# The order of work in a fused recurrence and MLP: first units from the third on, and the repeated unit

## The chip, the cores and the metric

The kernel runs on one core of a Trainium2 chip. The metric is the time of one execution on the device in microseconds (us); of several executions the median is taken. The five engines are called TensorE (PE in the profile; PEld is its loading of weights), VectorE (DVE), ScalarE (ACT), GpSimd (POOL) and SyncE (SP). Each works off its own instructions in the order in which the program issues them. Transfers are issued from the queues of SP, ScalarE and GpSimd, each in order too.

## The reference

Two blocks follow each other. The first is a recurrence over 768 time steps, for 4 batches and 8 heads of size 48, with a gate for every element of the key:

```
f = 1 / (1 + exp(-f_logit))
for t in range(S):
    state = f[t, :, None] * state + outer(k[t], v[t])      # 48 x 48 for each batch and head
    y[t]  = q[t] @ state
```

The heads' outputs are laid side by side to x of shape 4 x 768 x 384. The second block is a layer norm without offset and an MLP with a residual:

```
xn  = (x - mean) / sqrt(var + 1e-6) * g_ln
out = x + relu(xn @ w_ch1) @ w_ch2          # 384 -> 1536 -> 384
```

Everything is in float32 but the two weight matrices, which arrive as 64-bit floats; the kernel turns them into 32-bit ones on the chip.

## The kernel before

**Units.** Time is cut into 12 units of 64 steps. A unit holds all four batches, so 256 tokens, and all eight heads. `attention(n)` makes x of unit n, `mlp(n)` its result. The recurrence inside a unit becomes matrix products: running products of the gates forwards and backwards (two scans on VectorE), keys and queries multiplied by them, scores between them with a causal mask, scores times values, and the queries times the state that the earlier units left.

**Stages of attention**, each a name in the plan, with n the unit:

- gates (L691): sigmoid of the gates on ScalarE. For units 0 to 2 TensorE transposes the raw gates first. From unit 3 on (`DIRECT`) the data comes transposed by a transfer: `split` (words p and P, L421) copies the raw data on ScalarE into two planes of 16-bit halves and writes them to DRAM, and `transfer` (word x, L443) reads them back transposed, always on SP's queue. The tile `turned` takes the gates and later the queries of a unit.
- after and upto (L666, L675): the two scans; k and q (L712, L721): the keys times after (kh), the queries times upto (qh); kept (L732): the state times the unit's total gate.
- carried (L749, products at L758): queries times kept state, into the PSUM tile py; scores (L772) and causal (L778).
- kt (L788): kh transposed. From unit 3 on this is a transfer on SP that reads the halves of kh (word with K), which ScalarE (L440) and the queue have written before.
- values (L808): masked scores times v, added into py, and three copies on ScalarE that make x (L817, L819). chunk (L846): kt times v, the new part of the state, into the PSUM tile `shared`, which the scores use as well. state (L854): the sum of kept state and new part, on VectorE.
- stats, norm (L831 to L835, L876): mean and variance, and xn. turn (L887, L889): six transposes of xn on TensorE and six copies on ScalarE that multiply by g_ln and make xt.

**The MLP in steps.** `mlp(n)` is a generator, and each word m runs one step. In unit 0 the first product is made in halves by `first_half` (words h). Units 0 to 2 multiply plainly by w1 (L1023), units 0 and 1 plainly by w2 (L1033, six steps each). From unit 3 on the first product is made of 15 block products (`by_blocks`, L952), with sums of blocks of xt (`sums_of_x`, word y, L922, on VectorE) and sums of blocks of w1 (`mix_first`, words u for VectorE and U for GpSimd, L612, 13 steps in all). From unit 2 on the second product is made of seven products (L1052, named p1, p2, p6, p5, p7, p3, p4 in their order) with sums of blocks of h (`sums`, word s, L931 to L934) and of w2 (`mix`, words t and T, L586). Each product is followed by additions on VectorE and GpSimd (L1060) and by stores of results on SP. A unit from 3 on thus has 22 steps m.

**Weights.** Words f, r and w fetch a piece of a weight matrix (SP), unpack it (ScalarE, L547) and put it together (VectorE L556 to L561, GpSimd L563).

**Loads.** l and L load one of f, k, q, v of a unit, on SP's queue or ScalarE's, in four transfers (L475).

**What sets the order.** There is no planner at run time. Two strings hold it: START for the first units and UNIT, which is repeated for m = 3 to 11 with n = m + 1, o = m + 2, p = m + 3, z = m + 4. `run` goes through the words and issues each one's instructions; that order is every engine's order. Words of units that do not exist are passed over.

**PSUM.** py and shared have two banks each; the other four banks (`one_bank`) serve all other products and transposes in turn.

**A second path** (`general_path`) stands behind a condition for very small gates and is not taken with the reference's inputs.

## Time and profile before

| | |
|---|---|
| time, median of 3 runs | 431.71 us (430.95 to 435.05) |
| the profiled execution's own time | 433.26 us |
| its span, first to last instruction | 431.6 us |
| mean granted clock of TensorE | 0.992 |
| HBM read, written | 28.31 MB, 23.59 MB |

The page's first part gives each engine's busy time, its share of the span and its instructions. Its second part cuts the span into 40 slices of 10.8 us, a digit being the busy tenths. The waits name the engine and line that stood idle, what ended the wait, the sum in us, how often, and the longest. The chain of waits starts from the last instruction and goes back to what released it, or to the instruction before it on the same engine; in order of time it gives start, length and what it was. In a timeline each line is a start, a length, the engine, the line of the program, the operation, the tile written and the tiles read, the shape and the number of instructions; in brackets the idle time before it and what ended it. Queue lines (SPq, POOLq) are the issuing of transfers, not the transfers themselves. Lengths of neighbouring matmul groups overlap a little, since matmuls are pipelined.

### The profile page before, as it was taken

Reading aid. Unit: us, or ns where it says so; the run is one execution under the profiler, and the core shown is the slowest. Engines: PE = TensorE matmul, PEld = TensorE weight load, DVE = VectorE, ACT = ScalarE, POOL = GpSimd, SP = SyncE. Lnnn points to the kernel's source line nnn. Section 1 sums busy time; section 2 is a strip of 40 time slices with the busy share of each in tenths; the row PEclk is TensorE's granted clock in tenths of the full one; section 3 lists DMA queues with packets and bytes.
Section 4 is the critical chain, followed back from the end, with each engine's and each line's share of the span. In section 5 each row is a group of like instructions: output and inputs, shape, how many; then the busy total and the mean of one; then the engine's idle time right before and its main releaser. Section 6 shows DMA issues by size and latency. Waiting matters only on the chain.

```text
span 431.6 us, 12972 instructions
## 1 busy us (share of the span) xinstructions
PE 415.2 (96%) x5435; PEld 387.3 (90%) x5435; DVE 335.1 (78%) x539; ACT 215.3 (50%) x364; POOL 121.9 (28%) x148
## 2 busy tenths in 40 slices
PE   6599899999999999999999999999999999999994
PEld 5489787767879999999999999999999999999994
DVE  5999699769397779879879879878879878574561
ACT  2593786355243574573573573574583453341410
POOL 2351445832014115016016016025025024021020
PEclk9699999999999999999999999999999999999999
DMA  9998989857968698796796897897885782301001
GB/s 166 294 179 209 226 231 239 200 150 181 225 156 209 156 221 209 190 211 177 194 211 169 180 238 177 199 195 210 163 203 157 155 144 67 69 3 27 11 9 33
DMA packets 167647, 71.68 MB, mean 166 GB/s; under 512 B 151760, under 2 KB 157840, under 8 KB 167584
## 3 DMA queue, kind: packets, MB, share of 16 engines
q1 hardware_dynamic: 151728, 54.38, 58.4%
q0 software_dynamic: 3872, 12.64, 8.1%
q10 hardware_dynamic: 11984, 3.79, 4.2%
q8 instruction: 44, 0.72, 0.7%
q14 instruction: 19, 0.16, 0.1%
HBM read 28.31 MB, written 23.59 MB: 120 GB/s over the span
## 4 chain that ended last, share of the span: by engine, by line
PE 89%; DMA 4%; ACT 2%; DVE 2%; issue 1%; SPq 0%; ACTq 0%
PE pp L1052 32%; PE bx L952 11%; PE by L952 10%; PE ph L1023 7%; PE po L1033 7%; PE bz L952 4%; DMA w_0words<-in_moe_w_ch_dram 3%; PE py L808 3%; PE py L758 2%; PE shared L772 2%; PE ph L901 2%; PE bw L952 2%; PE bv L952 2%; PE xp L887 2%; PE shared L846 2%; DMA fraw<-in_f_logit_dram 1%
## 5 line engine op out<-in xcount | busy, mean ns | idle before, releaser
L963 ACT ACTIVATE h<-h 128x512 f32<-128x512 f32 x45 | 28.4, 630 | 42.0 <-DVE h L960 35.9
L1052 PE MATMUL pp<-mixed,h 128*128 128x192 f32 x240 | 42.3, 326 | 0.0
L1052 PE MATMUL pp<-w,h 128*128 128x192 f32 x240 | 40.9, 327 | 0.0
L1052 PE MATMUL pp<-mixed,s 128*128 128x192 f32 x240 | 40.6, 326 | 0.0
L1052 PEld LDWEIGHTS pp<-mixed,s 128*128 128x128 f32 x240 | 39.3, 190 | 0.0
L1052 PEld LDWEIGHTS pp<-w,h 128*128 128x128 f32 x240 | 38.8, 190 | 0.3
L1052 PEld LDWEIGHTS pp<-mixed,h 128*128 128x128 f32 x240 | 39.1, 190 | 0.0
L960 DVE TENSOR_TENSOR h<-h,bx 128x512 f32<-128x512 f32 x36 | 24.6, 683 | 18.1 <-PE bx L952 17.4
L669 DVE TENSOR_TENSOR_SCAN after<-gates,ends 128x1040 f32<-128x1040 f32 (+1 forms) x13 | 30.4, 2338 | 6.3 <-ACT gates L700 3.2
L440 ACT COPY Kplanes<-kh 128x1024 uint16<-128x1024 uint16 x18 | 18.1, 1044 | 34.2 <-DVE kh L717 31.1
L889 ACT ACTIVATE xt<-xp,gain 128x128 f32<-128x128 f32 x72 | 20.0, 378 | 28.9 <-PE xp L887 28.9
L1033 PE MATMUL po<-w,h 128*128 128x384 f32 x96 | 32.2, 487 | 0.0
L1023 PE MATMUL ph<-xt,w 128*128 128x256 f32 x144 | 31.8, 380 | 0.2 <-ACT xt L889 0.2
L1023 PEld LDWEIGHTS ph<-xt,w 128*128 128x128 f32 x144 | 27.2, 190 | 4.3 <-ACT xt L889 0.5
L834 POOL TENSOR_SCALAR rstd<-mv 128x2 f32<-128x2 f32 (+1 forms) x13 | 8.2, 627 | 76.3 <-DVE mv L832 76.1
L952 PE MATMUL bx<-y,v 128*128 128x128 f32 x216 | 28.9, 276 | 0.5 <-issue 0.4
L681 DVE TENSOR_TENSOR_SCAN upto<-gates,starts 128x1040 f32<-128x1040 f32 (+1 forms) x13 | 28.1, 2159 | 0.5
L1033 PEld LDWEIGHTS po<-w,h 128*128 128x128 f32 x96 | 17.9, 190 | 11.0
L441 POOL DMA_DIRECT2D qhalves<-qplanes x9 | 4.9, 544 | 79.5 <-ACT qplanes L440 79.5
L952 PEld LDWEIGHTS bx<-y,v 128*128 128x128 f32 x216 | 26.4, 192 | 0.8 <-issue 0.8
L563 POOL TENSOR_TENSOR w<-w_0upper,w_0units 128x768 int32<-128x768 int32 x7 | 15.0, 2139 | 25.6 <-DVE w_0upper L561 25.6
L440 ACT COPY kplanes<-kraw 128x1024 uint16<-128x1024 uint16 x18 | 18.1, 1045 | 8.0 <-DMA fhalves<-fplanes 3.2
(172 smaller groups left out, 962.7 us busy)
## 6 DMA issues: line engine op xcount, KB each, us to landing
w_0words<-in_moe_w_ch_dram SPq DMA_DIRECT2D x7, 768.0 KB, 6.4
v<-in_v_dram SPq DMA_DIRECT2D x46, 96.0 KB, 3.8
Khalves<-Kplanes POOLq DMA_DIRECT2D x16, 256.0 KB, 3.7
kraw<-in_k_dram SPq DMA_DIRECT2D x40, 96.0 KB, 3.5
fhalves<-fplanes POOLq DMA_DIRECT2D x14, 256.0 KB, 3.7
kraw<-in_q_dram SPq DMA_DIRECT2D x36, 96.0 KB, 3.1
fraw<-in_f_logit_dram ACTq DMA_DIRECT2D x27, 96.0 KB, 3.0
khalves<-kplanes SPq DMA_DIRECT2D x9, 256.0 KB, 2.6
```

The costliest lines, as they stand in the source:

```text
L440: nc.scalar.copy(out=to, in_=src)
L563: nc.gpsimd.tensor_tensor(out=to.bitcast(I32), in0=upper, in1=units, op=ALU.add)
L669: nc.vector.tensor_tensor_scan(out=at["after"].rearrange(flat)[:, c0:c1][:, ::-1], data0=gt[:, c0 + 1:c1 + 1][:, ::-1], data1=ends.rearran ...
L681: nc.vector.tensor_tensor_scan(out=at["upto"].rearrange(flat)[:, c0:c1], data0=gt[:, c0:c1], data1=starts.rearrange(flat)[:, c0:c1], initi ...
L808: nc.tensor.matmul(py[half(b ^ r), r, e * D:(e + 1) * D], lhsT=sc[half(b), r, e], rhs=vt[half(b), g, 2 * a + r], start=n == 0 and e == 0, ...
L889: nc.scalar.mul(out=xt[:, m, g * P:(g + 1) * P], in_=pt[:, m], mul=gain[:, m:m + 1])
L952: nc.tensor.matmul(banks[bank][:, i], lhsT=right[:, i * P:(i + 1) * P], rhs=left, start=new and i == 0, stop=True, skip_group_check=True)
L960: nc.vector.tensor_tensor(out=out[to], in0=out[to], in1=bank, op=op)
L963: nc.scalar.activation(out=out[to], in_=out[to] if bank is None else bank, func=AF.Relu)
L1023: nc.tensor.matmul(ph[:, j], lhsT=w1[:, m, (i + j) * P:(i + j + 1) * P], rhs=xt[:, m], start=m == 0, stop=m == KD - 1)
L1033: nc.tensor.matmul(po, lhsT=h[:, i, g * P:(g + 1) * P], rhs=w2[:, i], start=i == 0, stop=i == KF - 1)
L1052: nc.tensor.matmul(pp, lhsT=a[:, i], rhs=b[:, i], start=i == 0, stop=i == KH - 1)
```

## The change

Both strings are put in another order. Of START everything up to the word w that follows the fifth m1 stays; from there on, beginning with the query stage of unit 2 (a2.q), the words stand differently: among others a2.q, the load of unit 4's v (l4v), the mixing steps (t, u, U) and the steps m0, m1, m2 have other places. In UNIT the state's products (a{n}.chunk) stand before the values (a{n}.values); a{o}.upto and one of the splits of f stand one step m away from where they stood; a{o}.k stands before a{o}.q; the load of q stands a step earlier and the statistics a step later; and at the end one of the two K splits stands behind the turn, which itself stands one step m earlier. The words themselves, and how often each occurs, are the same.

```diff
 h01 r a1.kx h01 a1.carried a1.k l2f a1.scores w r a1.kt h00 a1.causal a1.values f w l2k
 a1.stats h00 f r a1.chunk a2.gates h01 a1.norm a1.turn l3f a2.kx f P3f0 m1 w r a2.after
 a2.k p3f1 a2.upto a1.state r l3k f a2.kept m1 P3k1 w m1 m1 r w l2v m1 w
-                                                                        p3k0 f m1 r x3f
-a3.gates a2.q l3q m0 m0 a2.carried L4f a2.scores a2.kt w a2.causal x3k P3q1 m1 u T
-a3.after U P3q0 L4k a2.values x3q a2.chunk U P4f1 m1 a3.k U a2.stats a2.norm P3K0 m0 m0
-u a2.state P4k1 m0 u a2.turn P4k0 t p3K1 m0 m2 l4q p4f0 a3.upto l3v a3.kept u u p4q0
-p4q1 m2 a3.q m2 u x4f u t l5f m1 a3.carried a3.scores m2 a4.gates m2 a3.causal m2 m1
-a3.values a4.after x4k a3.kt s2 x4q P5f0 a4.k P5f1 a3.chunk u a3.stats a3.state L5k l5v
-m2 a3.norm m1 p5k0 a4.upto l6f a4.q U p5k1 m1 x5f P4K1 l4v m2 m2 m2 U a3.turn l5q
-a5.gates p4K0 y3 m2 a4.kept m2 m2
+a2.q p3k0 f r m1 x3f m0 l3q P3q1 m0 x3k a2.carried a2.scores a3.gates a2.kt m1 w
+a2.causal P3q0 L4f a2.values a3.after L4k T P4f1 u a2.chunk m0 U x3q U U P4k1 a2.stats a3.k
+a2.norm P3K0 u m0 m1 a2.state m0 a2.turn p3K1 u m0 P4k0 t p4f0 l4q l3v m2 a3.upto a3.kept p4q1
+u p4q0 u m2 a3.q u m1 m2 t m2 a3.carried l4v a3.scores x4f m2 a4.gates u a3.causal m2 m1 a3.kt
+l5f a3.values a4.after s2 x4k x4q a4.k a3.stats u P5f1 a3.chunk L5k P5f0 p5k1 a3.state a3.norm
+a4.upto l5v m2 m1 p5k0 a4.q l6f m1 x5f m2 a4.kept P4K1 m2 l5q m2 m2 U a3.turn U a5.gates m2
+p4K0 m2 y3
 """
 UNIT = """
 a{n}.kt a{n}.carried p{p}f1 a{o}.after a{n}.scores m{m} a{n}.causal m{m} m{m} m{m} P{o}q0 m{m}
-m{m} m{m} m{m} m{m} a{o}.upto m{m} p{o}q1 p{p}f0 m{m} m{m} m{m} x{o}k a{n}.values l{p}k
-a{n}.chunk m{m} a{n}.stats m{m} x{o}q s{m} p{p}k1 P{p}k0 L{z}f a{o}.q a{o}.k m{m} x{p}f m{m}
-m{m} l{p}q l{p}v a{n}.norm m{m} m{m} a{n}.state m{m} p{o}K1 p{o}K0 a{n}.turn a{o}.kept y{n}
+m{m} m{m} m{m} a{o}.upto m{m} m{m} p{o}q1 m{m} p{p}f0 m{m} m{m} a{n}.chunk x{o}k a{n}.values
+l{p}k m{m} x{o}q m{m} a{n}.stats s{m} p{p}k1 a{o}.k P{p}k0 L{z}f a{o}.q m{m} x{p}f l{p}q m{m}
+m{m} l{p}v a{n}.norm m{m} m{m} a{n}.state p{o}K0 a{n}.turn m{m} a{o}.kept p{o}K1 y{n}
 a{p}.gates m{m}
 """
```

The lines are broken here where the two orders part; in the file the line breaks differ, the words do not.

## The prediction

> **What bounds the kernel now.** I read the page's busy rows first, then TensorE's waits (of the whole run, then from 84 us on), then the chain of waits in order of time.

> ```profile
> span 431.6 us, 12972 instructions
> PE 415.2 (96%) x5435; PEld 387.3 (90%) x5435; DVE 335.1 (78%) x539; ACT 215.3 (50%) x364; POOL 121.9 (28%) x148
> PE   6599899999999999999999999999999999999994
> ...
> PE shared L772 <- DVE qh L688: 5.2, 2, 3.7
> ...
> PE bx L952 <- issue: 0.4, 1, 0.4
> ...
> 206.34 1.08 PE py L758 x64
> 238.94 1.08 PE py L758 x64
> 270.92 1.08 PE py L758 x64
> 302.90 1.08 PE py L758 x64
> 335.26 1.08 PE py L758 x64
> 412.29 13.67 PE pp L1052 x84
> ```

> The third line is TensorE in 40 slices: the holes are at both ends. The longest wait, 5.2 us, belongs to the first units (line 688 serves only units 0 to 2). Asked from 84 us on, the view holds one line, the 0.4 us for the issue of a product. The chain says the same: from there on it runs over TensorE without a break, and the carried products (L758) that open each unit follow each other by 32.60, 31.98, 31.98 and 32.36 us. A unit is thus 31.98 us of TensorE work end to end, and two of these four are longer, by 0.62 and 0.38 us: 1.0 us in all, the 0.4 within it. The last product ends at 412.29 + 13.67 = 425.96, and the span's other 5.6 us are a last addition and a store.

> From where does the change act? The first word that differs is a2.q, ahead of unit 1's sixth product pair.

> ```profile
> 70.60 1.04 PE L661 MATMUL tr<-ident,qraw 128*128 128x128 f32 x8
> 72.26 1.28 DVE L688 TENSOR_TENSOR qh<-tr,upto 128x512 f32<-128x512 f32 x2
> 76.73 1.15 PE L758 MATMUL py<-kept,qh 48*64 48x48 f32 x64
> ```

> Its transposes stand at 70.60 us and move up by one product pair. Everything earlier, with nearly all of TensorE's idle time, keeps its order; what lies behind is TensorE from end to end. **No instruction is added or taken away: every word of both strings is there as often as before.** So the change can win back about 1.0 us at most, and can lose whatever wait it puts in front of TensorE.

> **The change, part by part.**

> *a2.q first.* On VectorE the queries' product stands behind a weight piece's conversion (w) in either order, at 72.26, and the carried products that need it come at 76.73, behind two products of unit 0 in either order: about 3 us of cover behind its end. Cost 0.

> *State's products (a{n}.chunk) ahead of the values, in the repeated unit.*

> ```profile
> 284.74 1.15 PE L808 MATMUL py<-v,sc 64*64 64x48 f32 x64
> 285.71 0.90 PE L846 MATMUL shared<-v,kt 64*48 64x48 f32 x64
> 286.54 1.16 PE L952 MATMUL by<-y,v 128*128 128x128 f32 x8
> 287.54 1.06 PE L952 MATMUL bx<-y,v 128*128 128x128 f32 x8
> 286.25 0.46 ACT L817 COPY x<-py 128x384 f32<-128x384 f32 x1
> 286.72 0.96 ACT L819 COPY x<-py 64x384 f32<-64x384 f32 x2
> 288.35 0.55 DVE L831 BATCH_NORM_STATS2 stats<-x 128x6 f32<-128x384 f32 x1
> ```

> The two groups stay neighbours behind the same 13 products. The 0.1 us that a group takes longer after a change of the tile's shape (1.16 against 1.06 for L952) falls on whichever comes first: 0, and at most 0.1 us a unit either way. The values end 0.83 us later (285.71 to 286.54), and ScalarE's copies of x with them. Those end now at 286.72 + 0.96 = 287.68 and the statistics start at 288.35, a cover of 0.67 us; but the first copy starts at 286.25, 0.5 us after the values gave way to the next group at 285.71, so some 0.4 of the 0.83 arrives. Cost 0; with the cover gone 0.2 us of VectorE a unit.

> *a{o}.k before a{o}.q; the load of q past a step.* The two products swap on VectorE and what follows them starts as now. On SP the four loads go ahead of two stores of results for which nothing waits. Cost 0.

> *The turn (transposes of the normalised x, L887) one product earlier, K1 behind it.* This shortens a cover. TensorE and VectorE in two units, and xn in an early one:

> ```profile
> 266.20 2.11 PE L1052 MATMUL pp<-w,s 128*128 128x192 f32 x12
> 264.96 1.13 DVE L876 TENSOR_SCALAR xn<-x,mv,rstd 128x384 f32<-128x384 f32 x2
> ...
> 298.18 2.11 PE L1052 MATMUL pp<-w,s 128*128 128x192 f32 x12
> 296.55 1.14 DVE L876 TENSOR_SCALAR xn<-x,mv,rstd 128x384 f32<-128x384 f32 x2
> 300.13 0.82 PE L887 MATMUL xp<-ident,xn 128*128 128x128 f32 x6
> ...
> 90.82 0.87 DVE L876 TENSOR_SCALAR xn<-x,mv,rstd 128x384 f32<-128x384 f32 x2 [2.39 <-POOL rstd L835]
> ```

> The transposes take the places at 266.20 and 298.18. xn is complete at 264.96 + 1.13 = 266.09 and at 297.69, so the cover shrinks, in the second unit from 300.13 - 297.69 = 2.44 us to 0.49, in the first to 0.11. The first three transposes need only xn's first half, which gives some 0.5 us more. I take 0.05 us for each of eight full units, 0.4 in all; the ends are 0 and 8 x 0.3 = 2.4 us, 0.3 being what xn is seen to vary by (0.87 there, 1.13 here). In return the copies of xt start 2 us ahead of now, which is worth 0 because y, made from them, is not late now. K1's copy falls behind the six xt copies, some 3 us:

> ```profile
> 299.12 1.41 POOL L441 DMA_DIRECT2D Khalves<-Kplanes  x2
> Khalves<-Kplanes POOLq DMA_DIRECT2D x16, 256.0 KB, 3.7
> 307.68 2.57 SPq L455 DMA_TRANSPOSE kt<-Khalves  x1
> ```

> The second half, issued at about 302.5 and landed 3.7 us later, is there at 306, and kt reads it at 307.68, on SP behind stores. Cost 0; were it late, SP would wait, behind it q's halves and the keys' transfer, and the state's products, which now come 13.8 us after the unit's opening (284.74 - 270.92), would lose of the 9 us that they come behind kt's issue.

> *The rest of START* moves products of units 0 to 2 against attention. The tight place is unit 4's gates: their transfer (x4f) now stands on SP behind a store of unit 1 and the four loads of unit 4's v.

> ```profile
> 108.37 0.55 DVE L1038 TENSOR_TENSOR x<-x,po 128x384 f32<-128x384 f32 x1 [0.51 <-PE po L1033]
> 102.36 2.77 SPq L475 DMA_DIRECT2D v<-in_v_dram  x4
> 106.03 2.91 SPq L455 DMA_TRANSPOSE turned<-fhalves  x1
> DMA to landing us min/median/max: 6.0/6.0/6.0
> turned<-fhalves SPq DMA_TRANSPOSE x9, 4.4
> 113.68 1.05 ACT L696 ACTIVATE gates<-turned 128x1024 f32<-128x1024 f32 x1
> 118.99 0.96 DVE L931 TENSOR_TENSOR s<-h 128x768 f32<-128x768 f32 x1 [1.91 <-ACT h L1025]
> 133.27 0.54 DVE L1038 TENSOR_TENSOR x<-x,po 128x384 f32<-128x384 f32 x1
> 135.70 0.82 PE L887 MATMUL xp<-ident,xn 128*128 128x128 f32 x6
> ```

> The store's addition (108.37, after 0.51 us of waiting for its product, which comes earlier now) stands behind as much VectorE work as now, so at about 107.9 and done at 108.4. About 1 us for the store and 2.8 for the loads (as at 102.36): x4f at 112 and landed, 6.0 us later as the one at 106.03 was, at 118; gates done at 119, now at 114.73. From there VectorE has the list it has now, up to the addition that ends at 133.27 + 0.54 = 133.81: 19.1 us, of which 1.9 are the wait at 118.99, which the delay swallows. So it is done at 119 + 17.2 = 136.2. It frees the PSUM bank of unit 2's product p7 (my reading, if banks go out in the order in which they come free), and p7 takes the transposes' place at 135.70. Cost 0.5 us; ends 0 (landing after 4.4 us, the median of the nine) and 2 us.

> **The sum.** The profiled execution took 433.26 us, 431.6 of span and 1.7 around it, and lies 1.55 us above the median of 431.71. 433.26 + 0.4 + 0.5 = 434.2, on the median's scale 432.6. The ends: 1.0 us of waits gone and nothing added, 430.7; both upper ends, 431.7 + 2.4 + 2.0 = 436.1.

> **The rivals.** One more row, the repeated unit in a window of 30 us (TensorE, weight loading, VectorE, ScalarE, GpSimd busy; clock; DMA):

> ```profile
> 230.00:260.00 30.00, 30.00 (x455) 29.51 (x455) 25.31 (x44) 18.25 (x30) 7.16 (x11) 1.00 0.83 189
> ```

> *VectorE's lag reaches TensorE in every unit (slower).* The turn now stands in front of a product, and all VectorE work ahead of xn is on its path. For: a cover of 0.11 us, and VectorE busy 25.3 us in 30. From a lag of 0.85 us on it decides: past the covers of 0.11 to 0.49 us, eight units lose over 0.5 us each, 4.3 us and more: 436. Against: but for k and q, VectorE's order up to xn stays. Chance 0.10. [...]

> *START leaves a gap (slower, under 1%).* x4f lands late, or ScalarE, which works in order, waits for a load with a relu behind it: 1 to 3 us once, 433 to 435. Chance 0.15.

> *TensorE has room that the order frees (faster).* Then units fall below 31.98 us; 0.55 us in each of eight is 4.4 us: 427. Against it: TensorE busy 30.00 and weight loading 29.51 of 30 us, units alike to 0.01 us. Chance 0.02. [...]

> *The change does nothing on the clock*: both groups of products were covered before and after, 431.7. This is the forecast's lower half.

> **How the numbers follow.** Forecast with its lower half 0.73, START's gap 0.15, VectorE's lag 0.10, freed room 0.02. Predicted: 432.1, the middle between nothing (431.7) and my sum (432.6). The three runs shown lie between 430.95 and 435.05, so the range adds a few tenths to its case: 430.4 to 434.8 holds the forecast and START's gap for the most part. About 1% is what a measurement of this kernel can tell from no change: faster 0.03, within 0.86, slower 0.11.

> **What would show it.** Right: TensorE's waits from 84 us on stay under 1.5 us, units open 31.98 us apart, L887 has a wait for xn of at most 0.3 us a unit. A line of L887 waiting for DVE xn with eight entries means the first rival; a wait of L1052 between 130 and 140 us, or gates of unit 4 after 119, means START; units below 31.9 us would prove my bound wrong. Wrong as a whole: a time below 430 or above 436.

## The result and the profile after

| | before | after |
|---|---|---|
| median | 432.01 us (430.45 to 435.05, 20 runs) | 435.76 us (433.02 to 438.90, 20 runs) |
| ratio | | 1.0076 (95% interval 1.0055 to 1.0097) |
| the profiled execution's own time, span | 433.26, 431.6 us | 435.68, 433.9 us |

The change makes the kernel 0.76% slower, some 3.3 us: a loss clear of the noise, within 1% of no change, and above the forecast's 432.1 and its range. The profiled executions of e4_m1_first (442.26 us) and h2_xf_behind_lq (468.59 us) below were slow ones, so lengths read from them are rough. Line numbers after are one lower than before (L1038 is L1037, L758 is L757). First the page of the kernel after: span, busy time, TensorE's slices, and one of the DMA queues (packets, MB, share of 16 engines' time).

```profile
span 433.9 us, 12958 instructions
PE 415.2 (96%) x5435; PEld 387.0 (89%) x5435; DVE 332.4 (77%) x539; ACT 215.8 (50%) x364; POOL 122.7 (28%) x148
PE   6599899999999999999999999999999999999994
q8 instruction: 44, 0.72, 0.7%
```

TensorE's 415.2 us of work are those of before, so the time went into its pauses. Its waits after, from 70 us on:

```profile
PE pp L1051 <- DVE x L1037: 0.8, 1, 0.8
PE ph L1022 <- DVE x L1037: 0.7, 1, 0.7
PE bx L951 <- issue: 0.5, 1, 0.5
PE py L807 <- issue: 0.5, 1, 0.5
```

Before, there was one such line, 0.4 us of issue. Two kinds are new or grown: a wait for VectorE's last addition of a unit (L1037), twice, and pauses that end in nothing the profile names ("issue"). They lie in different stages, which the carried products that open each unit show. From the timelines, unit 2, unit 4 and unit 11 before:

```profile
76.73 1.15 PE L758 MATMUL py<-kept,qh 48*64 48x48 f32 x64
142.30 1.15 PE L758 MATMUL py<-kept,qh 48*64 48x48 f32 x64
367.17 1.15 PE L758 MATMUL py<-kept,qh 48*64 48x48 f32 x64
```

and unit 2 and then 4 to 11 after:

```profile
75.79 1.15 PE L757 MATMUL py<-kept,qh 48*64 48x48 f32 x64
143.41 1.15 PE L757 MATMUL py<-kept,qh 48*64 48x48 f32 x64
175.39 1.15 PE L757 MATMUL py<-kept,qh 48*64 48x48 f32 x64
207.68 1.15 PE L757 MATMUL py<-kept,qh 48*64 48x48 f32 x64
240.47 1.15 PE L757 MATMUL py<-kept,qh 48*64 48x48 f32 x64
272.45 1.15 PE L757 MATMUL py<-kept,qh 48*64 48x48 f32 x64
305.19 1.15 PE L757 MATMUL py<-kept,qh 48*64 48x48 f32 x64
337.38 1.15 PE L757 MATMUL py<-kept,qh 48*64 48x48 f32 x64
369.37 1.15 PE L757 MATMUL py<-kept,qh 48*64 48x48 f32 x64
```

From unit 2 to unit 4, all in START's order, 65.57 us became 67.62: **2.05 us**. From unit 4 to unit 11, in UNIT's, 224.87 became 225.96: **1.09 us**. (The timeline's starts lie up to 0.1 us off those of the chain that the prediction shows.) Together 3.1 us, near the 3.3 of the ratio (the medians themselves lie 3.75 apart). (The two spans differ by only 2.3: the profiled execution of before reached unit 2 0.94 us later. Over all runs here that point lies between 75.3 and 76.7 us wherever no products are added ahead of it; why was not looked into.)

### The profile page after: what moved, and what is told of

It reads as the page before. It is cut to its first block, busy times and chain, and to the rows that moved or that the text cites. A ratio compares the mean times of both kernels' runs of the same rounds, so it can differ in the third digit from the quotient of the medians.

```text
span 433.9 us, 12958 instructions
## 1 busy us (share of the span) xinstructions
PE 415.2 (96%) x5435; PEld 387.0 (89%) x5435; DVE 332.4 (77%) x539; ACT 215.8 (50%) x364; POOL 122.7 (28%) x148
## 2 busy tenths in 40 slices
PE   6599899999999999999999999999999999999994
## 4 chain that ended last, share of the span: by engine, by line
PE 91%; DVE 2%; DMA 2%; ACT 2%; issue 1%; DVEq 0%; ACTq 0%
PE pp L1051 32%; PE bx L951 11%; PE by L951 10%; PE ph L1022 7%; PE po L1032 7%; PE bz L951 4%; PE ph L900 3%; PE py L807 3%; PE py L757 3%; PE shared L771 3%; PE bw L951 2%; PE bv L951 2%; PE shared L845 2%; PE xp L886 2%; DMA w_0words<-in_moe_w_ch_dram 1%
## 5 line engine op out<-in xcount | busy, mean ns | idle before, releaser
L1051 PEld LDWEIGHTS pp<-mixed,s 128*128 128x128 f32 x240 | 39.2, 190 | 1.1 <-DVE x L1037 1.1
L1022 PE MATMUL ph<-xt,w 128*128 128x256 f32 x144 | 32.2, 381 | 0.9 <-DVE x L1037 0.7
L439 ACT COPY Kplanes<-kh 128x1024 uint16<-128x1024 uint16 x18 | 19.1, 1059 | 27.0 <-DMA khalves<-kplanes 20.4
L1032 PE MATMUL po<-w,h 128*128 128x384 f32 x96 | 32.2, 487 | 0.0
L1022 PEld LDWEIGHTS ph<-xt,w 128*128 128x128 f32 x144 | 27.0, 190 | 5.6 <-issue 1.3
L888 ACT ACTIVATE xt<-xp,gain 128x128 f32<-128x128 f32 x72 | 20.0, 376 | 23.9 <-PE xp L886 23.9
L439 ACT COPY fplanes<-fraw 128x1024 uint16<-128x1024 uint16 x18 | 18.7, 1041 | 14.5 <-DMA qraw<-khalves 6.2
## 6 DMA issues: line engine op xcount, KB each, us to landing
Khalves<-Kplanes POOLq DMA_DIRECT2D x16, 256.0 KB, 3.0
fhalves<-fplanes POOLq DMA_DIRECT2D x14, 256.0 KB, 4.1
khalves<-kplanes SPq DMA_DIRECT2D x9, 256.0 KB, 3.3
```

The lines of the kernel that those rows point to most:

```text
L439: nc.scalar.copy(out=to, in_=src)
L888: nc.scalar.mul(out=xt[:, m, g * P:(g + 1) * P], in_=pt[:, m], mul=gain[:, m:m + 1])
L1022: nc.tensor.matmul(ph[:, j], lhsT=w1[:, m, (i + j) * P:(i + j + 1) * P], rhs=xt[:, m], start=m == 0, stop=m == KD - 1)
L1032: nc.tensor.matmul(po, lhsT=h[:, i, g * P:(g + 1) * P], rhs=w2[:, i], start=i == 0, stop=i == KF - 1)
L1051: nc.tensor.matmul(pp, lhsT=a[:, i], rhs=b[:, i], start=i == 0, stop=i == KH - 1)
```

## The experiments

Each kernel is compared with the kernel before, run on the same chip. Two lengths are read from every trace: **START's**, from unit 2's carried products to unit 4's (65.57 before, 67.62 after), and **UNIT's**, from unit 4's to unit 11's (224.87 and 225.96).

### START and UNIT apart

```diff
 e1_start_only: the kernel before with the changed START
 e2_unit_only:  the kernel before with the changed UNIT
```

> START in the new order, UNIT in the old one. Theory S (the loss sits in START: in the changed kernel's trace unit 2's first product waits 0.74 us for the addition at the end of unit 0, and its product p5 0.80 us for unit 1's last addition, each with 0.2 us of a restart): ratio to before about 1.0045 (+2 us), both waits still there, units as long as before. Theory U (the loss is made in the repeated unit, by TensorE's pauses at the state's products and values): ratio about 1.000 to 1.002.

> START in the old order, UNIT in the new one. Theory S: no wait for L1037 before 140 us, ratio about 1.000 to 1.0025, what is left being pauses of the kind 'issue' in units 4 to 11. Theory U: ratio about 1.005 to 1.0075, and the carried products of successive units stand more than 32.2 us apart on the mean (31.98 when nothing waits).

e1: 434.24 us, ratio 1.0038 (1.0017 to 1.0059); START 67.76 us, UNIT 224.72. e2: 433.52 us, 1.0024 (1.0002 to 1.0047); START 65.57, UNIT 227.08, and no wait for L1037. Each half costs something by itself, in the place that the profile after showed. (UNIT alone loses 2.21 us in e2's trace, where the whole change lost 1.09: one execution of each.)

### START: whose bank

In e1 the timeline of TensorE has the two waits again:

```profile
97.44 5.42 PE L1022 MATMUL ph<-xt,w 128*128 128x256 f32 x24 [0.74 <-DVE x L1037]
134.56 2.22 PE L1051 MATMUL pp<-mixed,s 128*128 128x192 f32 x12 [0.94 <-DVE x L1037]
```

The programs built from the kernels name each product's PSUM bank, and so tell whose bank is waited for: which product gets which bank follows from the order of the words. After, unit 2's first product (the row at 97.44) takes the bank of unit 0's last product, whose addition VectorE can only begin when TensorE has just finished it; before, it took another one. And unit 2's fourth product p5 (134.56) takes the bank of unit 1's last product; before, unit 3's transposes took it, which stood right behind p5 (at 135.70 in the prediction's rows). Two kernels take away what makes them wait, one each:

```diff
 e3_l4v_back: the kernel after, unit 4's v loaded where it was before
-a3.carried l4v a3.scores x4f
+a3.carried a3.scores x4f
...
-P4K1 m2 l5q
+P4K1 l4v m2 l5q
 e4_m1_first: the kernel after, unit 1's ninth step ahead of unit 2's first
-l4q l3v m2 a3.upto a3.kept p4q1 u p4q0 u m2 a3.q u m1 m2
+l4q l3v m1 m2 a3.upto a3.kept p4q1 u p4q0 u m2 a3.q u m2
```

> The changed kernel with one word moved: the load of unit 4's v stands behind P4K1 again, as before, and so no longer ahead of the transfer of unit 4's gates on SP. Theory S, its second half: gates of unit 4 about 2.8 us earlier than 117.28 us, unit 2's p5 no longer waits for the addition at L1037, about 1.0 us gained on the changed kernel (ratio to before 1.005 instead of 1.0076). If p5 waits all the same, the transfer was not what made VectorE late. Theory U: no change, 1.0076.

> The changed kernel with unit 1's ninth step put ahead of unit 2's first one, so that TensorE has 2.6 us of other work between the end of unit 0 and the product whose PSUM bank that addition frees. Theory S, its first half: the 0.74 us wait of L1022 for L1037 near 97 us goes, about 0.9 us gained on the changed kernel (ratio 1.0055), the wait of p5 stays. If another wait takes its place there, the bank was not the whole cause. Theory U: no change, 1.0076.

e3: 434.75 us, 1.0044 (1.0026 to 1.0062); p5's wait is gone, the other stays at 0.74 us (this view puts it down to ScalarE, though the addition of L1037 ends just before it here too), START 66.55. e4: 435.13 us, 1.0041 (1.0018 to 1.0065); the wait at unit 2's first product is gone, but p5 waits. Then both together, with UNIT as before:

```diff
 e6_both_oldunit: START with both edits, UNIT as before
```

> The changed START with two words put back (unit 4's values' load behind the keys' split; unit 1's ninth product step ahead of unit 2's first), the repeated unit as before. Theory B (all that START loses are the two waits of TensorE for a PSUM bank that a last addition of VectorE frees): no wait for the addition (L1037) is left, carried products of unit 2 to unit 4 65.4 to 65.8 us apart (before 65.57, START changed 67.76), ratio 0.999 to 1.001. Rival: START's other moves cost as well: 66 us and more, ratio 1.002 to 1.004.

432.63 us, ratio 0.9998 (0.9978 to 1.0018): START's loss is gone from the times. START's length missed its figure, 66.71 us instead of 65.4 to 65.8, by one row:

```profile
133.39 2.22 PE L1051 MATMUL pp<-mixed,s 128*128 128x192 f32 x12 [0.85 <-DVE x L1037]
```

Without the first wait, TensorE reaches p5 earlier, and the second one is back. Times and trace do not agree here: the trace keeps 1.14 us of START's loss, 0.26%, and the interval of the ratio ends at 0.18%. In the traces of after, e1, e3 and e6 START is 65.57 us plus, for each of the two waits that is left, its idle time and some 0.25 us that no row names: 0.74 makes 66.55, 0.85 makes 66.71, 0.74 and 0.80 make 67.62. So nothing else that START's order costs shows in these lengths.

### UNIT: TensorE runs out of instructions

The pauses of kind "issue" in the kernel after, and the one before had:

```profile
209.80 1.16 PE L952 MATMUL bx<-y,v 128*128 128x128 f32 x8 [0.35 <-issue]
```

```profile
211.41 1.16 PE L951 MATMUL bx<-y,v 128*128 128x128 f32 x8 [0.54 <-issue]
288.64 0.33 PE L807 MATMUL py<-v,sc 64*64 64x48 f32 x7 [0.50 <-issue]
```

The last falls between product 57 and 58 of a group of 64 that need nothing new. Counted in the trace over all of TensorE's records (products, weight loads and its few waits for semaphores, some 45 up to the first pause), in order of start, the three begin at instruction 5313, 5313 and 7617, which is 449 + 256 x 19 and 449 + 256 x 28. The page's queue q8 carries 44 transfers of 16,384 bytes: one for each 256 such instructions, 64 bytes each. In the records of the transfers, number 19 or 28 of that queue lands 1.50, 1.30 and 1.52 us before the pause ends. By this TensorE waits for its own instructions there. Of the 39 pauses of at least 0.15 us from unit 4 to the last products, in all kernels of this study but h2 below, 37 begin at 449 + 256 i and end 1.2 to 1.7 us behind the landing of transfer i. (Some of them the view of waits puts down to ScalarE.)

Whether it is the count or (theory D) the work at this place was tried by shifting the count: small products more in unit 0, far ahead. The trace has two records, and two weight loads, for each such product.

```diff
 h1_shift144 (36 products, UNIT as changed), h3_old_shift224 (56, UNIT as before), h4_new_shift224 (56, UNIT as changed); START as before
         def do_scores(gs=both):
...
+            for _ in range(36 if n == 0 and gs[0] == 1 else 0):
+                nc.tensor.matmul(ps[half(0), 0, NP], lhsT=ident[0:T, 0:T], rhs=ident[0:T, 0:T],
+                                 start=True, stop=True)
```

> START as before, the repeated unit as changed, and 36 small products (64x64, 144 TensorE instructions in the trace's count: each is two products and two weight loads) more in unit 0, where TensorE waits 3.7 us for the queries; they write a place that unit 0's scores overwrite. Theory I (TensorE runs out of its own instructions, which come 256 at a time: all pauses so far start at instruction 449 + 256 i): every boundary moves 144 instructions ahead in the work. The boundaries that now fall at the end of the dense pair of state's products and values lie in units 4, 7 and 10 (the blocks that end there take 1.9, 2.3 and 2.8 us against some 3 for a transfer), so units 4 and 7 take 32.5 to 33.5 us, and units 5, 6, 8 and 9 take 31.98 to 32.1 (with the unit changed and nothing added: 32.47, 32.67, 33.23, 32.74). Rival theory D (the pauses belong to the work of these units: a buffer, a load or VectorE that comes late there): units 5, 6, 8 and 9 stay as long as they were.

> The kernel before with 56 small products more in unit 0 (224 TensorE instructions, 2 us where TensorE waits 3.7 us), nothing else. Theory I: the pauses of units 6 and 9 (0.62 and 0.38 us before) go; the blocks that end in the dense pair of units 5 and 8 take 2.2 and 2.6 us, about what a transfer takes there, so 0 to 0.4 us each; carried products of unit 4 to unit 11 223.9 to 224.6 us apart (before 224.87), ratio 0.997 to 1.001. Theory D: units 6 and 9 as before, 224.9.

> START as before, the repeated unit as changed, and the 56 small products more. Theory I: of the four pauses (2.2 us in the units' time) one is left, in unit 5, where the block takes 2.7 us and a transfer 2.9 to 3.8: carried products of unit 4 to unit 11 224.1 to 225.3 us apart (with the unit changed and nothing added 227.08), units 6, 8 and 9 within 0.2 us of 31.98, ratio 0.998 to 1.002. Theory D: 226.5 to 227.5 us and a ratio of 1.002 to 1.003.

Their times (444.18, 444.48 and 443.60 us; ratios 1.0198, 1.0266 and 1.0250) say nothing of units, since the added products took 0.11 us a record, not the 0.018 that I had taken from the scores; in h4, 111 records took 12.10 us:

```profile
16.01 12.10 PE L768 MATMUL shared<-ident 64*64 64x64 f32 x111 [2.54 <-DVE sc L786]
```

The units say what was asked. h1: units 5, 6, 8 and 9 take 31.98 us each, all their pauses gone; unit 7 takes 33.87 us (32.5 to 33.5 expected), unit 10 32.27, and unit 4, where as much was expected as in unit 7, 31.98. h3: units 6 and 9, which had the pauses before, are at 31.98, units 5 and 8 at 33.06 and 32.98. h4: 33.36 and 33.25 in units 5 and 8, the rest 31.98. The new pauses, one row for each of h1, h3 and h4:

```profile
269.00 0.60 PE L954 MATMUL by<-y,v 128*128 128x128 f32 x3 [1.63 <-issue]
```

```profile
201.65 0.72 PE L954 MATMUL by<-y,v 128*128 128x128 f32 x5 [0.92 <-issue]
```

```profile
201.68 0.71 PE L954 MATMUL by<-y,v 128*128 128x128 f32 x4 [1.11 <-issue]
```

begin at instruction 449 + 256 x 25, x 18 and x 18. The pauses moved with the count, in either order of the unit, so theory D is out. My sizes were off: in h3 1.0 us came in units 5 and 8 where 0 to 0.4 were expected, and in h4 unit 8 kept a pause of 1.1 us where none was. From unit 4 to unit 11 the three kernels take 226.06, 225.95 and 226.51 us, so no shift tried beats the 224.87 of the kernel before.

Most boundaries cost nothing. In the traces of before and after, from number 12 on, all blocks of 256 instructions but four took TensorE 5.7 to 19.8 us, and it stood idle at the end of none of these. Blocks 17, 19, 28 and 30 took 2.7 to 3.6 us with their pauses, and every pause at a boundary, up to 0.54 us, lies at the end of one of these four. They are the blocks that hold most of two neighbouring groups of small products (values and state's products in units 5 and 8, carried products and scores in 6 and 9): with their weight loads the 128 products of such a pair make up as many instructions as a block, and they run through in 1.8 us (188.18 to 189.98 in unit 5 before). The transfers themselves took 0.9 to 1.6 us in these two traces, and from a landing to the end of the pause it was 1.3 to 1.6 us. In h1 the pause behind such a pair reached 1.63 us.

### UNIT: what makes the transfer late

Transfers 17 and 28 belong to units 5 and 8, where a block ends inside these two groups. When they land, in us behind the unit's carried products, and what the two units lose against 31.98 us each, worked out from the transfers' records and the carried rows of each trace:

```
                      q, k   state's    landing    landing   lost in
                      order  products   unit 5     unit 8    5 and 8
before                q k    behind     13.13      13.51     0.01
e1_start_only         q k    behind     12.96      13.29     0.01
e6_both_oldunit       q k    behind     12.79      13.23     0.00
j2_old_own            q k    behind     12.82      13.43     0.00
j3_only_chunk_first   q k    ahead      12.78      13.84     0.00
g1_unit_qk_back       q k    ahead      12.90      13.96     0.00
g2_only_k_first       k q    behind     13.40      14.02     0.01
g3_unit_chunk_back    k q    behind     13.92      14.18     0.27
j1_unit_own           k q    ahead      13.75      14.42     0.52
j4_chunk_and_k        k q    ahead      14.16      14.38     0.84
after                 k q    ahead      14.03      14.67     1.07
e4_m1_first           k q    ahead      14.45      14.55     1.25
k2_unit_again         k q    ahead      14.34      14.97     1.46
k1_unit_own_again     k q    ahead      14.36      14.37     1.52
e3_l4v_back           k q    ahead      14.41      15.06     1.63
e2_unit_only          k q    ahead      14.33      15.29     1.74
```

Past some 14.0 us a landing costs, nearly microsecond for microsecond; up to then hardly anything. (0.3 of k1's 1.52 are another wait.) The figure fits the trace of before: TensorE there needs the first instruction of the block 15.41 us behind the carried products in unit 5 and 15.45 in unit 8, and it goes on 1.2 to 1.7 us behind a landing. The two units make up 1.07 of the 1.09 us that UNIT lost after. Units 6 and 9, where the pauses of before lie, lose 0.4 to 1.9 us together in these traces, in either order; so UNIT's length in a single execution can lie 1 us off.

What moves is the start of the transfer. It takes 0.9 to 1.5 us in all these rows, and TensorE enters the block ahead of it in unit 5 at the same point, 12.2 to 12.6 us behind the carried products; but the transfer starts there at 11.5 to 12.0 us with the queries' product first and at 12.3 to 13.3 with the keys' first. The single edits behind the table, each a word or two of UNIT, START as before:

```diff
 g1_unit_qk_back: UNIT as changed, but
-a{o}.k P{p}k0 L{z}f a{o}.q m{m}
+P{p}k0 L{z}f a{o}.q a{o}.k m{m}
 g2_only_k_first: UNIT as before, but
-P{p}k0 L{z}f a{o}.q a{o}.k m{m}
+a{o}.k P{p}k0 L{z}f a{o}.q m{m}
 g3_unit_chunk_back: UNIT as changed, but
-a{n}.chunk x{o}k a{n}.values l{p}k
+x{o}k a{n}.values l{p}k a{n}.chunk
 j3_only_chunk_first: UNIT as before, but
-x{o}k a{n}.values l{p}k a{n}.chunk
+a{n}.chunk x{o}k a{n}.values l{p}k
 j4_chunk_and_k: UNIT as before with the edits of g2 and j3
```

> START as before, the repeated unit as changed, but with the queries' product (a{o}.q) ahead of the keys' (a{o}.k) again, the only word put back. Theory SP (the queries' product 1.2 us later holds back the next gates' transfer, which needs its buffer, and with it SP and the loads behind it, into which TensorE's own instruction transfers then run): the gates' transfer (L454 into turned) comes about 7.5 us ahead of the unit's carried products again, not 6.4, the pauses of kind 'issue' on TensorE sum to at most 0.7 us instead of 2.2, carried products of unit 4 to unit 11 lie 224.9 to 225.5 us apart (before 224.87, unit-only 227.08), ratio 1.000 to 1.001. Rival theory G (the swap of state's products and the values, or the turn, makes the pauses by itself): 226.5 to 227.5 us and a ratio of 1.002 to 1.003, as with the whole unit changed.

> The kernel before with one word moved: in the repeated unit the keys' product (a{o}.k) ahead of the split of the keys and of the queries' product. Theory SP: the gates' transfer comes about 6.4 us ahead of the unit's carried products instead of 7.5, pauses of kind 'issue' on TensorE of 1 to 2.5 us in all, carried products of unit 4 to unit 11 226 to 227.5 us apart, ratio 1.001 to 1.003. Theory G: nothing, 224.9 us and a ratio of 0.999 to 1.001.

> START as before, the repeated unit as changed, but with state's products behind the values again, the only word put back. Theory SP: no better than the unit as changed: 226.5 to 227.5 us from unit 4's carried products to unit 11's, pauses of about 2 us, ratio 1.002 to 1.003. Theory G, if it is the swap of the two groups: pauses of at most 0.7 us, 224.9 to 225.5 us, ratio 1.000 to 1.001.

> The kernel before with one word moved: in the repeated unit state's products ahead of the values. Theory SP: the instruction transfers of units 5 and 8 land at 12.8 to 13.9 us behind the carried products as before, both units take 31.98 to 32.1 us; 224.5 to 225.4 us from unit 4's carried products to unit 11's, ratio 0.999 to 1.001. Theory K: landing past 14.0, 225.6 us and more, ratio 1.001 to 1.003.

> The kernel before with two words moved in the repeated unit: state's products ahead of the values, and the keys' product ahead of the queries'. Theory SP: the delay comes through the second alone, so the instruction transfers of units 5 and 8 land where they did with that word alone, at 13.4 to 14.2 us, and the two units together take 0 to 0.4 us more than 63.96; 224.3 to 225.6 us from unit 4's carried products to unit 11's. Theory K, in which both words are needed: they land at 14.0 to 15.3 us, and it is 226 to 227.5 us, as with the whole unit changed.

Ratios: g1 1.0020 (1.0000 to 1.0039), g2 1.0002 (0.9981 to 1.0024), g3 1.0022 (1.0005 to 1.0040), j3 1.0014 (0.9984 to 1.0043), j4 1.0000 (0.9974 to 1.0025). These times can't be told apart at this size, and j4's does not follow its profile; the verdicts go by the traces, one profiled execution each. UNIT's lengths: g1 225.34, g2 224.24, g3 225.45, j3 224.78, j4 225.70; those of g2 and g3 are well below what theory SP, explained below, had said (226 us and more). With the queries' product first, no kernel loses anything in units 5 and 8; with the keys' first, all but one do. That word is needed. It seems not to be enough: alone (g2) it brings the landing to the edge only, and together with the state's products ahead (j4) over it, as theory K (both words are needed) had it and SP not. The step from g2 to j4, 0.4 and 0.8 us, is no larger than what two profiled executions of one kernel can differ by (j1 and k1 below: 0.6 us in unit 5), so this rests on the table as a whole: with the keys' first, 0.01 and 0.27 us are lost with the state's products behind, 0.52 to 1.74 with them ahead.

How it acts stayed open. My theory SP was that the next gates' transfer waits for the queries' product, which reads the same buffer (`turned`), and SP with it. This part is so: in units 5 to 9 of the kernel after, the transfer is issued 0.7 to 1.9 us later in the unit than before, and the keys' transfer, behind it on SP, 1.1 to 1.8 us later. What followed was tried with a buffer of its own for the gates' transfer:

```diff
 j1_unit_own, k1_unit_own_again (UNIT as changed), j2_old_own (UNIT as before); START as before
             turned["f"] = turned["q"] = work.tile([P, NS, T], FP32, name="turned")
+        if name == "f" and n == DIRECT + 1:
+            turned["f"] = late["pool"].tile([P, NS, T], FP32, tag="turnedf", name="turnedf")
```

> START as before, the whole repeated unit as changed, but from unit 4 on the gates' transfer has a buffer of its own instead of the one that the queries' product reads, so that it no longer waits for that product; TensorE's instructions and banks and VectorE's order are those of the unit as changed. Theory SP: the gates' transfer comes at least 7.5 us ahead of the unit's carried products (with the unit changed 6.4), the keys' transfer (L454 into qraw) has been issued by 11.5 us behind them (12.2), the instruction transfers of units 5 and 8 land by 13.9 us, both units take 31.98 to 32.15 us; carried products of unit 4 to unit 11 224.5 to 225.6 us apart (227.08), ratio 0.999 to 1.002. Rival theory K (what the swapped groups or the turn do to TensorE itself, not SP's delay, makes the transfers late): they land at 14.0 to 15.3 us as with the unit changed, 226.5 to 227.5 us, ratio 1.002 to 1.004.

> The kernel before with the gates' transfer in a buffer of its own, nothing else. Theory SP: SP is earlier than before, but units 5 and 8 have no pause to lose, and the pauses of units 6 and 9 lie 3.5 us behind the carried products, where SP's keys' transfer has not begun: 224.0 to 225.2 us from unit 4's carried products to unit 11's (before 224.87), ratio 0.997 to 1.001. Theory K: the same.

> The unit as changed with the gates' transfer in a buffer of its own, a second look: in the first the profiled execution showed little loss in the units (225.49 us from unit 4's carried products to unit 11's, pauses of 0.8 us in all), yet the timed ones a ratio of 1.0074. If the early transfer costs something of its own (in the first profile ScalarE stands 37 us, up to 8.5 us at a time, in front of the split of K, for the write of the k halves out of the buffer that it needs), the ratio is 1.005 to 1.010 again and a slower execution shows TensorE waiting for what ScalarE makes (L888 to L890, L697) in some unit. If the first times were chance: 0.999 to 1.003.

> START as before, the repeated unit as changed, a second look on the same chip as the own buffer: 226.5 to 227.5 us from unit 4's carried products to unit 11's with all pauses at instruction 449 + 256 i, ratio 1.001 to 1.005. If the first profile (227.08) was chance: 224.7 to 225.5 us and a ratio of 0.999 to 1.001.

j1: 435.13 us, 1.0074 (1.0045 to 1.0102), UNIT 225.49; k1, the same kernel: 435.48 us, 1.0061 (1.0033 to 1.0090), UNIT 226.89; k2, e2's kernel on the same chip as k1: 433.86 us, 1.0032 (1.0008 to 1.0055), UNIT 226.78; j2: 432.68 us, 1.0012 (0.9986 to 1.0038), UNIT 225.82. j2's UNIT missed its 224.0 to 225.2 us through units 6 and 9. k1 shows the first profile of j1 to have been a lucky one: the loss is there. Whether the own buffer costs something of its own the times leave open (k1's interval overlaps k2's), and TensorE's waits for the turn or the gates, expected for that case, don't show. ScalarE's waits from 140 to 370 us in k1, first line:

```profile
ACT Kplanes L439 <- DMA khalves<-kplanes: 36.3, 6, 9.0
```

It stands 36 us, up to 9.0 at a time, for the write of the keys' halves; with the shared buffer it was 9.6 us in k2. The own buffer did not bring SP's keys' transfer back: in unit 5 it is issued 8.71 us behind the carried products in j1 and 10.42 in k1, against 7.71 before and 8.84 after. So these kernels tell against the buffer alone, not against SP's lateness. For that there is a sign: in 14 of the table's 16 traces the instruction transfer of unit 5 starts 1.3 to 1.8 us behind the end of SP's issue of the keys' transfer, in either order (0.3 and 0.4 us in k1 and e2; in unit 8 the distance varies more). But no kernel moved SP alone by the right amount, so what delays the instruction transfer with the keys first is not settled. k2 repeats e2's loss, in the times and in the trace.

One more kernel was to delay SP alone:

```diff
 h2_xf_behind_lq: the kernel before, but in UNIT
-x{p}f m{m} m{m} l{p}q
+m{m} m{m} l{p}q x{p}f
```

> The kernel before with one word moved: in the repeated unit the gates' transfer (x{p}f) behind the loads of the queries (l{p}q) on SP. TensorE's order and VectorE's stay. Theory SP+I: the gates' transfer and what SP has behind it, up to the keys' transfer, run 1 to 2 us later; TensorE's instruction transfer in units 5 and 8 starts behind the keys' transfer and lands 14.0 to 15.5 us after the unit's carried products (before 13.1 and 13.5; the pauses so far begin where it lands past 13.9), so that these two units take 0.2 to 1.5 us more each; carried products of unit 4 to unit 11 225.3 to 227.5 us apart, ratio 1.001 to 1.005. Rival theory K (the order of the keys' and the queries' product, or the swap of the two groups on TensorE, is needed for it): units 5 and 8 stay at 31.98 us.

465.91 us, ratio 1.0730 (1.0681 to 1.0778). It tells nothing about instructions, because the dose was too large: the edit put the gates' transfer behind a store of results as well, in front of which SP waits for VectorE's additions (first line of SP's waits from 140 to 400 us in h2),

```profile
SPq L1064 <- DVE p L1059: 33.2, 7, 8.1
```

and the gates' transfer for the next unit (rows of h2 and of before) comes 2.7 us ahead of that unit's carried products at 287.69, where it came 7.9 us ahead of those at 302.83: over 5 us later, not 1 to 2.

```profile
284.98 3.34 SPq L454 DMA_TRANSPOSE turned<-fhalves  x1
```

```profile
294.91 1.78 SPq L455 DMA_TRANSPOSE turned<-fhalves  x1
```

From 140 us on VectorE and TensorE wait in h2:

```profile
DVE after L668 <- ACT gates L695: 32.3, 6, 6.5
```

```profile
PE bx L951 <- ACT h L956: 16.2, 4, 4.8
PE bx L951 <- issue: 7.1, 2, 4.2
```

What it does show is the price of late gates: units 5 to 10 of 36.6 to 39.2 us.

## Why the prediction was wrong

The change costs some 3 us where the sum had 0.9: 0.86 on "within 1%" holds, but 432.1 with a range to 434.8 missed 435.76. Of the prediction's own signs, TensorE's waits from 84 us on came to 2.5 us, not under 1.5, and the wait between 130 and 140 us that was to mean START is there. By its steps:

- **What bounds the kernel** held: TensorE end to end, busy 415.2 us in both, at most 1.0 us to win, and none of it won.
- **a2.q first**: 0, held; no wait at unit 2's carried products.
- **State's products ahead of the values**: the groups cost what was forecast and the statistics start no later (17.5 us behind the carried products with and without, in j3 and before). What the step did not weigh is that the pair is where TensorE's instructions run dry.
- **a{o}.k before a{o}.q, "what follows them starts as now"**: this step failed. It cost 1.1 us after and 1.7 in e2 where 0 stood: with the keys' product first (and the state's products ahead) the instruction transfers of units 5 and 8 land past the point from which they cost, and with this one word put back (g1) nothing is lost there. The gates' transfer reads into the buffer that q reads, so it and what SP issues behind it move with q; that this is what delays the instructions stays open. I had the four loads and two stores in view and not the buffer.
- **The turn one product earlier**, 0.4 us with an upper end of 2.4: mis-sized. No wait of L886 for xn is in the profile after; it measured 0. Of the K split behind it no cost shows either.
- **The rest of START**, 0.5 us with an upper end of 2: one wait of this kind came, but the bank was read wrongly, and a second wait was left out. The rows of after (SP, ScalarE, VectorE, TensorE):

```profile
106.80 1.17 SPq L1039 DMA_DIRECT2D out_dram<-x  x2
108.07 2.76 SPq L474 DMA_DIRECT2D v<-in_v_dram  x4
110.93 2.69 SPq L454 DMA_TRANSPOSE turned<-fhalves  x1
```

```profile
117.28 1.06 ACT L695 ACTIVATE gates<-turned 128x1024 f32<-128x1024 f32 x1 [0.88 <-DMA turned<-fhalves]
```

```profile
97.08 0.55 DVE L1037 TENSOR_TENSOR x<-x,po 128x384 f32<-128x384 f32 x1 [2.86 <-PE po L1032]
134.15 0.54 DVE L1037 TENSOR_TENSOR x<-x,po 128x384 f32<-128x384 f32 x1
```

```profile
97.78 5.42 PE L1022 MATMUL ph<-xt,w 128*128 128x256 f32 x24 [0.74 <-DVE x L1037]
134.75 1.57 PE L1051 MATMUL pp<-mixed,s 128*128 128x192 f32 x8 [0.80 <-DVE x L1037]
```

Store, loads, transfer, gates done at 118.3 (119 said), last addition done at 134.7 (136.2 said): each came, a little earlier than said. But that addition frees the bank of p5, not of p7, so it is waited for sooner, and costs 1.05 us with the 0.25 behind it. The other wait, at 97.78, was not in the working at all: VectorE waits 2.86 us for the very product whose bank TensorE needs next. START thus cost 2.05 us where 0.5 stood.

The rival "START leaves a gap" named unit 4's gates behind the loads and 433 to 435, which is where e1's 434.24 lies; e3 shows that half. The wait at 97.78 has another cause and came on top, and UNIT's loss was in no rival. "VectorE's lag reaches TensorE in every unit" is out, by the missing wait of L886. No room was freed either: after, the units from 4 to 10 take 31.98 to 32.79 us each. The share of weight loading, 90% before and 89% after, hardly sees 3 us of pauses.

The sum then: 0.4 + 0.5 stood for 2.05 in START and 1.1 to 2.2 in UNIT (after 1.09, e2 2.21).

## What to carry to other kernels

When the order of products changes, work out again which bank, and which buffer, each of them takes: a pool that hands them out as they come free ties a product to another one than before, and a product that needs the bank of the one just finished waits for the addition between them (0.74 us here). Count TensorE's instructions as a resource: here the stretches in which 256 of them pass in 1.8 us were fragile, with 1.1 us for the transfer of a block and 1.2 to 1.7 us from its landing to the end of a pause, and small moves elsewhere decided whether it showed (0.00 to 1.74 us lost in units 5 and 8). And a few tenths of a per cent need the trace's own lengths, several executions of them, since timed ratios with an interval of 0.2% each way did not separate single words here.
